# Attention scores from two fp32r parts of q and k in place of fp32 operands

## The chip, the cores and the metric

The kernel runs on one core of one Trainium2 chip. The metric is the device time of one execution in microseconds (us). The engines are TensorE (PE, with its weight loads listed apart as PEld), VectorE (DVE), ScalarE (ACT), GpSimd (POOL) and SyncE (SP), which here only issues DMAs. Each engine works through its own instructions in order.

## What is computed

Attention over 4 batches, 8 heads, 576 positions and a head size of 64, followed by a feed-forward layer over the 2304 tokens (512 to 2048 to 512).

```python
scores = q @ k.T / sqrt(64)
scores = scores + bias[head]          # a small network of log1p(|i-j|)/log1p(max(i,1)), one per head
attn = exp(scores - max) / (sum + 1e-9)
x = attn @ v                          # then laid out as 2304 x 512
h = x @ w_in
out = (s * relu(h)**2 + b) @ w_out    # w_in, w_out come as 64-bit floats
```

Everything is float32. The inputs q, k, v, w1, b1, w2 and w_in are drawn 8 times larger than the reference first draws them.

## The kernel before, in words

The order of all instructions is written out by hand (`tc.manual_schedule()`): what stands later in the program stands later in its engine's queue. There are three stages.

**Bias.** 36 steps compute the biases of 16 rows each, for all heads. The features of step st + 2 are issued ahead of step st (L118 is POOL's part of them), PE sums them (L135, L138), ACT evicts them (L142) and SP stores them to DRAM (L143). A table, `plan`, adds loads to single steps: among others q and k of pair 1 at step 6, q of pair 2 at step 20 and k of pair 2 at step 23. At steps 33 and 35 it starts the first two score units. Before those, the last biases are loaded back (L161, L162, L164), and SP waits there until their stores have landed.

**Attention.** The work is cut into 16 pairs: one head and two batches, whose 64-row q and k lie on partitions 0 to 63 and 64 to 127 of one tile (`qt`, `kt`, 128x640). A pair has five units. Units 0 to 3 are 128 query rows of both batches: `scores` (L196) makes four matmuls, two halves of 288 keys for each batch on its own 64 rows of the array. Unit 4 holds the last 64 rows of both batches and makes two matmuls on all 128 rows. The scores lie in a ring of two PSUM tiles (`sps`).

`step(n)` runs a pipeline of two units and one pair. In program order: scores and bias (DVE, L212) of unit n+2; the divisors of unit n+1 on DVE (L231, L232) and its scaling on POOL (`norm_scale`, L237); the transposes of unit n on PE (L259, L250, or L268, L263 in unit 4), which wait for that scaling, each evicted by ACT (L260, L255) or DVE (L257, L265); the exponentials of unit n+2 on ACT (L221); a fifth of attn @ v of the pair before (L283, L286); and, from pair 1 on, one `fill()`. Then come loads: q and k three pairs ahead at unit 3 (L171, L177), v at unit 4, and biases at unit 2 of every second pair.

`fill()` takes the next piece of decoding one weight block. A block has five pieces and a pair five steps, so the pieces keep their places. At unit 0: for the blocks that are split at once, a cast on DVE (L341) and a subtraction on POOL (L344), both of the block before, and then the absolute value on ACT (L322). At unit 1: a clip on POOL (L324). At units 2 to 4: DVE (L326, L329, L332). The blocks split at once are the first eight, so L344 runs in pairs 2 to 9.

**Feed-forward.** x and the weights are split into two fp32r parts, and expand (L379) and project (L408) sum three fp32r passes: high x high, high x low and low x high. During the first 512 tokens the rest of the weights is decoded.

The change touches `load_q`, `load_k`, `scores`, `step` and `plan`.

Of the kernel before, what the change touches and what calls it, by code (L numbers as in the profile page):

```python
# [9 lines left out]
F32 = mybir.dt.float32  # L10
F32R = mybir.dt.float32r
I32 = mybir.dt.int32
U32 = mybir.dt.uint32
AF = mybir.ActivationFunctionType
ALU = mybir.AluOpType
# [11 lines left out]
def attention_moe(ctx, tc, q, k, v, w_in, w_out, dist, par, out):  # L27
    nc = tc.nc
    NB, H, S, D = 2 * q.shape[0], q.shape[1], k.shape[3] - 64, q.shape[2] // 2
# [4 lines left out]
    HALF = S // 2  # L34
# [6 lines left out]
    NP = len(pairs)  # L41
    LAST = 5 * NP
# [7 lines left out]
    io = prep_ctx.enter_context(tc.tile_pool(name="io", bufs=2))  # L50
# [100 lines left out]
    qs, ks, vals, tts, bts, pts, units, accs = {}, {}, {}, {}, {}, {}, {}, {}  # L151
# [15 lines left out]
    def load_q(p):  # L167
        if p < NP:
            h, b0 = pairs[p]
            qs[p] = io.tile([128, 640], F32, tag="qt", name="qt", bufs=3)  # L170
            nc.sync.dma_start(out=qs[p], in_=q[b0 // 2, h])  # L171

    def load_k(p):
        if p < NP:
            h, b0 = pairs[p]
            ks[p] = io.tile([128, S + 64], F32, tag="kt", name="kt", bufs=3)
            nc.sync.dma_start(out=ks[p], in_=k[b0 // 2, h])  # L177

    def load_v(p):
        if p < NP:  # L180
            h, b0 = pairs[p]
            vt = tp.tile([128, 10 * D], F32, tag="vn", name="vt")
            nc.sync.dma_start(out=vt, in_=v[b0 // 2, h])
            vals[p] = vt.rearrange("p (i d) -> p i d", d=D)

    def scores(n):
        p, t = divmod(n, 5)
        qt, kt = qs[p], ks[p]
        c = slice(128 * t, 128 * t + 128)
        xs = range(width(n))  # L190
        ps = [ps_s.tile([128, 2, 512], F32, tag="s", name="sps") for _ in xs]
        for hf in range(2):
            for x in xs:
                d = slice(64 * x, 64 * x + 64) if t < 4 else slice(0, 128)
                o = hf * HALF + (64 if x == 0 else 0)
                nc.tensor.matmul(  # L196
                    ps[x][:, hf, 0:HALF], qt[d, c], kt[d, o:o + HALF], start=True, stop=True)
        units[n] = (
            tp.tile([128, 2, S], F32, tag="pr", name="pr"),
            sm.tile([128, 2], F32, tag="mn", name="mn"),  # L200
            sm.tile([128, 2], F32, tag="su", name="su"),
            sm.tile([128, 2], F32, tag="rs", name="rs"),
            ps,
        )

    def biased(n, x):
        p, t = divmod(n, 5)
        _, mn, _, _, ps = units[n]
        bt, be = bts[group[p]]
        bias = bt[:, t, 64 - 64 * x:64 - 64 * x + S] if t < 4 else be  # L210
        tt = tp.tile([128, S], F32, tag="tt", name="tt")
        nc.vector.tensor_tensor_reduce(  # L212
            tt.rearrange("p (a b) -> p a b", a=2), ps[x][:, :, 0:HALF],
            bias.rearrange("p (a b) -> p a b", a=2),
            -1.0 / ROOT, BIG, ALU.add, ALU.min, mn[:, x:x + 1],
        )
        tts[n, x] = tt

    def expo(n, x):
        pr, mn, su, _, _ = units[n]  # L220
        nc.scalar.activation(  # L221
            pr[:, x], tts.pop((n, x)), AF.Exp, bias=mn[:, x:x + 1], scale=-1.0,
            accum_out=su[:, x:x + 1])

    def width(n):
        return 2 if n % 5 < 4 else 1

    def norm(n):
        _, _, su, rs, _ = units[n]
        c = slice(0, width(n))  # L230
        nc.vector.tensor_scalar(su[:, c], su[:, c], 1e-9, None, op0=ALU.add)  # L231
        nc.vector.reciprocal(rs[:, c], su[:, c])  # L232

    def norm_scale(n, x):
        pr, _, _, rs, _ = units[n]
        r = rs[:, x:x + 1]
        nc.gpsimd.tensor_scalar(pr[:, x], pr[:, x], r, 1.0, op0=ALU.mult, op1=ALU.mult)  # L237

    def probs_t(n, part):
        p, t = divmod(n, 5)  # L240
        pr = units[n][0]
        if p not in pts:
            pts[p] = (ptp.tile([128, 4, 2, S], F32, tag="pt", name="pt"),
                      ptp.tile([128, S], F32, tag="ptr", name="ptr"))
        pt, ptr = pts[p]
        ps = ps_t.tile([128, 512], F32, tag="t", name="tps")
        c = slice(128 * t, 128 * t + 128)
        if t < 4 and part < 2:
            for kb in range(4):
                nc.tensor.transpose(  # L250
                    ps[:, 128 * kb:128 * kb + 128],
                    pr[:, part, 64 * part + 128 * kb:64 * part + 128 * kb + 128], ident)
            o, i = pt[:, :, part, c], ps.rearrange("p (a b) -> p a b", a=4)
            if part == 0:
                nc.scalar.activation(o, i, AF.Copy)  # L255
            else:
                nc.vector.tensor_copy(o, i)  # L257
        elif t < 4:
            nc.tensor.transpose(ps[:, 0:128], pr.rearrange("p x j -> p (x j)")[:, 512:640], ident)  # L259
            nc.scalar.activation(ptr[:, c], ps[:, 0:128], AF.Copy)  # L260
        elif part == 0:
            for kb in range(4):
                nc.tensor.transpose(  # L263
                    ps[:, 128 * kb:128 * kb + 128], pr[:, 0, 128 * kb:128 * kb + 128], ident)
            nc.vector.tensor_copy(  # L265
                pt[:, :, :, 512:S], ps.rearrange("p (a x b) -> p a x b", a=4, x=2))
        else:
            nc.tensor.transpose(ps[0:64, 0:128], pr[:, 0, 512:S], ident)  # L268
            for x in range(2):
                nc.scalar.activation(  # L270
                    ptr[64 * x:64 * x + 64, 512:S], ps[0:64, 64 * x:64 * x + 64], AF.Copy)

    def av(p, kb, hf):
        h, b0 = pairs[p]
        pt, ptr = pts[p]
        vt = vals[p]
        if kb == 0 and hf == 0:
            accs[p] = ps_x.tile([128, 2, 512], F32, tag="x", name="xps")
        ps = accs[p]
        c = slice(hf * HALF, (hf + 1) * HALF)  # L280
        if kb < 4:
            for x in range(2):
                nc.tensor.matmul(ps[64 * x:64 * x + 64, hf, 0:HALF], vt[:, 4 * x + kb, :], pt[:, kb, x, c],  # L283
                                 start=(kb == 0), stop=False)
        else:
            nc.tensor.matmul(ps[:, hf, 0:HALF], vt[:, 8:10].rearrange("p i d -> p (i d)"), ptr[:, c],  # L286
                             start=False, stop=True)
        if kb == 4 and hf == 1:
            xs = tp.tile([128, S], F32, tag="xs", name="xs", bufs=1)
            nc.scalar.activation(xs.rearrange("p (a b) -> p a b", a=2), ps[:, :, 0:HALF], AF.Copy)  # L290
            nc.sync.dma_start(out=xt_d[b0 // 2][:, h * D:(h + 1) * D, :], in_=xs)
# [130 lines left out]
    def ok(n, x):  # L422
        return 0 <= n < LAST and x < width(n)
# [7 lines left out]
    def step(n):  # L431
        p, u = divmod(n, 5)
        m = n + 2
        cur = 0 <= n < LAST
        if ok(m, 0):
            scores(m)
            biased(m, 0)
        if ok(n + 1, 0):
            norm(n + 1)
            norm_scale(n + 1, 0)  # L440
            if ok(n + 1, 1):
                norm_scale(n + 1, 1)
        if ok(m, 1):
            biased(m, 1)
        if cur:
            for part in (2, 0, 1) if u < 4 else (1, 0):
                probs_t(n, part)
        if ok(m, 0):
            expo(m, 0)
        if ok(m, 1):  # L450
            expo(m, 1)
        if p >= 1:
            av(p - 1, u, 0)
            av(p - 1, u, 1)
            fill()
        if n < LAST:
            if u == 3:
                load_q(p + 3)
                load_k(p + 3)
            if u == 4:  # L460
                load_v(p + 2)
            for e in loads_at.get((p, u), ()):
                load_bias(*e)
# [14 lines left out]
    def fill():  # L478
        next(filler, None)
# [10 lines left out]
        6: ((load_q, 1), (load_k, 1)),  # L490
        11: ((load_bias, 0, 0, 1),),
        17: ((load_bias, 0, 1, 2),),
        20: ((load_v, 0), (load_q, 2)),
        23: ((load_k, 2), (load_v, 1)),
        26: ((load_bias, 0, 2, 3),),
        29: ((load_w, *early[0]),),
        32: ((load_w, *early[1]),),
# [41 lines left out]
    for n in range(LAST - 2):  # L539
        step(n)  # L540
        if n >= LAST - 10:
            fill()
        if n == LAST - 4:
            for _ in filler:
                pass
            for a in range(KB):
                load_x(0, a)
    prep_ctx.close()
    xp = ctx.enter_context(tc.tile_pool(name="xp", bufs=1, reuse_waits="tile"))
    op = ctx.enter_context(tc.tile_pool(name="op", bufs=2, reuse_waits="tile"))  # L550
# [24 lines left out]
    for i in range(2, len(todo) + LAG):  # L575
        if i < len(todo):
            c, f = todo[i]
# [83 lines left out]
```

## Time and profile before

| | us |
|---|---|
| median of three runs (766.27 to 768.84) | 767.32 |
| the profiled execution | 769.54 |
| its span, first to last instruction | 767.8 |
| bias stage and its loads, until the scores go on | 0 to 73.2 |
| attention, pairs of 17.17 each | 73.2 to about 322 |
| end of attention and first tokens of the feed-forward | about 322 to 421 |
| the other tokens | 421 to 767.8 |

A row of the page of groups reads: line, engine, operation, output and inputs by the program's names, shapes, count, then busy time and mean nanoseconds of one, then the idle time of the engine right before them and what ended it. A row of a timeline reads: start and length in us, engine, line, operation, count, and in brackets the idle time before it with its releaser. In the chain of waits a row is start, length and what held the end back then. The chain goes by what came last, so an engine can be on it for long and still be closely followed by another.

### The profile page before, as it was taken

What the parts mean: (1) busy time and instruction counts of PE and PEld (TensorE: products, weight loads), DVE (VectorE), ACT (ScalarE), POOL (GpSimd) and SP (SyncE); (2) the same over time, 40 slices, a digit from 0 to 9 for tenths busy, and PEclk for the clock granted to TensorE, in tenths of its full rate; (3) what the DMA queues carried; (4) which work ended last, traced back from release to release, by engine and by line L of the source; (5) the groups of instructions that cost most, each with busy time, mean ns of one, the idle gap of its engine ahead of it and who ended that gap; (6) DMA issues with size and microseconds to landing.
All of it is one profiled execution on the core that took longest, in us unless ns stands there. A gap on an engine that the chain in (4) does not pass through costs nothing.

```text
span 767.8 us, 11563 instructions
## 1 busy us (share of the span) xinstructions
PE 735.5 (96%) x4226; PEld 528.1 (69%) x4226; DVE 433.3 (56%) x874; ACT 383.5 (50%) x788; POOL 242.8 (32%) x290
## 2 busy tenths in 40 slices
PE   8985999999999999999887999999999999999998
PEld 4443566666666666657655888888888888888896
DVE  7973678778777777866888432223322323223332
ACT  7983667777666677765454432223222323222332
POOL 7952345455554444438867310000000000000000
PEclk9997999999999999999989999999999999999999
DMA  5896243535444541252333003000300002000100
GB/s 173 285 335 195 81 161 112 175 126 195 156 155 141 182 143 61 76 172 79 110 123 89 10 15 95 1 0 1 107 4 1 1 0 83 1 0 1 56 1 27
DMA packets 36056, 71.56 MB, mean 93 GB/s; under 512 B 7712, under 2 KB 10912, under 8 KB 36000
## 3 DMA queue, kind: packets, MB, share of 16 engines
q1 hardware_dynamic: 35856, 70.51, 27.8%
q8 instruction: 33, 0.54, 0.3%
q10 hardware_dynamic: 144, 0.33, 0.1%
q14 instruction: 23, 0.19, 0.1%
HBM read 50.77 MB, written 20.05 MB: 92 GB/s over the span
## 4 chain that ended last, share of the span: by engine, by line
PE 80%; DMA 5%; POOL 4%; DVE 4%; issue 3%; ACT 3%; SPq 0%; ACTq 0%; POOLq 0%; DVEq 0%
PE o L408 23%; PE hps L379 22%; PE sps L196 12%; PE xps L283 8%; PE tps L250 8%; PE bps L135 2%; DMA bias<-stg 2%; PE xps L286 2%; PE tps L259 2%; POOL gt L391 2%; ACT stg L142 1%; DMA be<-bias 1%; DVE full L326 1%; DMA xt<-xs 1%; POOL full L324 1%
## 5 line engine op out<-in xcount | busy, mean ns | idle before, releaser
L408 PE MATMUL o<-who,gt 128*128 128x512 f32 x576 | 196.6, 401 | 12.6 <-ACT gt L390 8.9
L379 PE MATMUL hps<-x,whi 128*128 128x512 f32 (+1 forms) x640 | 184.4, 373 | 0.0
L384 DVE SCALAR_TENSOR_TENSOR r<-r,sb 128x512 f32<-128x512 f32 (+1 forms) x80 | 63.2, 790 | 182.9 <-ACT r L383 182.9
L237 POOL TENSOR_SCALAR pr<-pr,rs 128x576 f32<-128x576 f32 x144 | 108.8, 768 | 152.9 <-DVE rs L232 96.6
L383 ACT ACTIVATE r<-hps 128x512 f32<-128x512 f32 (+1 forms) x80 | 44.4, 554 | 191.3 <-PE hps L379 191.1
L408 PEld LDWEIGHTS o<-who,gt 128*128 128x128 f32 x576 | 109.5, 191 | 42.0 <-ACT gt L390 11.1
L379 PEld LDWEIGHTS hps<-x,whi 128*128 128x128 f32 x640 | 117.2, 188 | 24.4 <-issue 0.4
L212 DVE CUSTOM_DVE_ANT_0 tt<-sps,bt 128x576 f32<-128x576 f32 x128 | 95.8, 749 | 43.8 <-PE sps L196 42.2
L379 PE MATMUL hps<-x,wli 128*128 128x512 f32 (+1 forms) x320 | 118.8, 371 | 0.0
L221 ACT ACTIVATE pr<-tt,mn 128x576 f32<-128x576 f32 x144 | 110.2, 768 | 14.8 <-DVE su L231 12.2
L196 PE MATMUL sps<-kt,qt 64*128 64x288 f32 (+1 forms) x576 | 107.9, 437 | 9.8 <-DVE mn L212 9.4
L408 PE MATMUL o<-wlo,gt 128*128 128x512 f32 x288 | 114.5, 398 | 0.0
L196 PEld LDWEIGHTS sps<-kt,qt 64*128 64x128 f32 (+1 forms) x576 | 61.2, 189 | 52.0 <-DVE mn L212 21.0
L250 PE MATMUL tps<-ident,pr 128*128 128x128 f32 x512 | 76.7, 282 | 0.0
L283 PE MATMUL xps<-pt,vt 128*64 128x288 f32 x512 | 75.8, 418 | 0.0
L394 DVE SCALAR_TENSOR_TENSOR gt<-r,sb,gt 128x512 fp32r<-128x512 f32 (+1 forms) x64 | 43.8, 684 | 47.3 <-ACT gt L393 47.3
L379 PEld LDWEIGHTS hps<-x,wli 128*128 128x128 f32 x320 | 60.2, 188 | 11.1
L393 ACT ACTIVATE gt<-r,sb 128x512 fp32r<-128x512 f32 (+1 forms) x64 | 42.9, 670 | 48.2 <-DVE r L384 48.2
L250 PEld LDWEIGHTS tps<-ident,pr 128*128 128x128 f32 x512 | 57.7, 142 | 12.1 <-ACT ptr L260 10.5
L408 PEld LDWEIGHTS o<-wlo,gt 128*128 128x128 f32 x288 | 55.0, 191 | 11.5
L283 PEld LDWEIGHTS xps<-pt,vt 128*64 128x64 f32 x512 | 31.2, 136 | 23.9 <-issue 10.8
L257 DVE COPY pt<-tps 128x512 f32<-128x512 f32 x64 | 43.9, 687 | 3.5 <-PE tps L250 3.3
(66 smaller groups left out, 751.3 us busy)
## 6 DMA issues: line engine op xcount, KB each, us to landing
bias<-stg SPq DMA_DIRECT2D x36, 288.0 KB, 4.0
raw<-in_moe_w_in_dram SPq DMA_DIRECT2D x16, 512.0 KB, 3.5
raw<-in_moe_w_out_dram SPq DMA_DIRECT2D x16, 512.0 KB, 8.6
bt<-bias SPq DMA_DIRECT2D x7, 1152.0 KB, 12.7
qt<-in_q_dram SPq DMA_DIRECT2D x16, 320.0 KB, 10.2
kt<-in_k_dram SPq DMA_DIRECT2D x16, 320.0 KB, 10.5
vt<-in_v_dram SPq DMA_DIRECT2D x16, 320.0 KB, 9.3
xt<-xs SPq DMA_DIRECT2D x16, 288.0 KB
```

Of the source, the lines that this page charges most:

```text
L196: nc.tensor.matmul(ps[x][:, hf, 0:HALF], qt[d, c], kt[d, o:o + HALF], start=True, stop=True)
L212: nc.vector.tensor_tensor_reduce(tt.rearrange("p (a b) -> p a b", a=2), ps[x][:, :, 0:HALF], bias.rearrange("p (a b) -> p a b", a=2), -1.0 ...
L221: nc.scalar.activation(pr[:, x], tts.pop((n, x)), AF.Exp, bias=mn[:, x:x + 1], scale=-1.0, accum_out=su[:, x:x + 1])
L237: nc.gpsimd.tensor_scalar(pr[:, x], pr[:, x], r, 1.0, op0=ALU.mult, op1=ALU.mult)
L250: nc.tensor.transpose(ps[:, 128 * kb:128 * kb + 128], pr[:, part, 64 * part + 128 * kb:64 * part + 128 * kb + 128], ident)
L257: nc.vector.tensor_copy(o, i)
L283: nc.tensor.matmul(ps[64 * x:64 * x + 64, hf, 0:HALF], vt[:, 4 * x + kb, :], pt[:, kb, x, c], start=(kb == 0), stop=False)
L379: nc.tensor.matmul(ps[:, 0:n], w[0, g][:, a, fc], xs_t[c, a][:, j, 0:n], start=(i == 0), stop=(i == 3 * KB - 1))
L383: nc.scalar.activation(r, ps[:, 0:n], AF.Relu)
L384: nc.vector.scalar_tensor_tensor(r, r, sb[:, 0:1], r, op0=ALU.mult, op1=ALU.mult)
L394: nc.vector.scalar_tensor_tensor(lo, r, sb[:, 1:2], hi.bitcast(F32), op0=ALU.add, op1=ALU.subtract)
L408: nc.tensor.matmul(os_t[c][i], gt[:, a, tok], w[1, g][:, fo], start=(f == 0 and j == 0), stop=(f == NF - 1 and j == 2))
```

## The change

Each pair's q and k are split after their load. ScalarE copies the tile as fp32r (the high part), and GpSimd subtracts the copy from the tile (the low part). The two parts lie in one tile of twice the size. `scores` makes three fp32r matmuls (high x high, high x low, low x high) in place of each fp32 matmul, ordered by half, then by pass, then by batch, so that neighbouring matmuls are on different 64 rows. The splits of pair p+1 stand at the end of the steps of units 0 (q) and 1 (k) of pair p, and those of pair 0 behind bias steps 30 and 31. The loads of q and k come two pairs ahead with two buffers, not three with three, and so leave bias steps 20 and 23.

```diff
+    def split_qk(p, which):
+        if p < NP:
+            full = (qs, ks)[which][p]
+            t = io.tile([128, 2, 640], F32R, tag=f"r{which}", name="qr" if which == 0 else "kr")
+            nc.scalar.activation(t[:, 0], full, AF.Copy)
+            nc.gpsimd.tensor_tensor(t[:, 1], full, t[:, 0].bitcast(F32), op=ALU.subtract)
+            (qs, ks)[which][p] = t
...
+        mms = []
         for hf in range(2):
             for x in xs:
                 d = slice(64 * x, 64 * x + 64) if t < 4 else slice(0, 128)
                 o = hf * HALF + (64 if x == 0 else 0)
-                nc.tensor.matmul(
-                    ps[x][:, hf, 0:HALF], qt[d, c], kt[d, o:o + HALF], start=True, stop=True)
+                for i, (a, b) in enumerate(((0, 0), (0, 1), (1, 0))):
+                    mms.append((i, hf, x, ps[x][:, hf, 0:HALF], qt[d, a, c], kt[d, b, o:o + HALF]))
+        for i, _, _, o, a, b in sorted(mms, key=lambda e: e[1::-1]):
+            nc.tensor.matmul(o, a, b, start=(i == 0), stop=(i == 2))
...
-        if n < LAST:
+        if 0 <= n < LAST:
             if u == 3:
-                load_q(p + 3)
-                load_k(p + 3)
+                load_q(p + 2)
+                load_k(p + 2)
+            if u < 2:
+                split_qk(p + 1, u)
...
-        20: ((load_v, 0), (load_q, 2)),
-        23: ((load_k, 2), (load_v, 1)),
+        20: ((load_v, 0),),
+        23: ((load_v, 1),),
+        30: ((split_qk, 0, 0),),
+        31: ((split_qk, 0, 1),),
```

The tiles `qt` and `kt` also go from three buffers to two.

## Rows read from the trace of the kernel before

**Rows 1.** The page: busy tenths of PE and POOL and the granted clock of PE, each in 40 slices of the span.

```profile
PE   8985999999999999999887999999999999999998
...
POOL 7952345455554444438867310000000000000000
PEclk9997999999999999999989999999999999999999
```

**Rows 2.** Busy time of the engines in stretches: a pair with the POOL subtraction of the weights, a pair without it. Columns: stretch, its length, then each engine's busy time and instructions, granted clock, DMA share and GB/s.

```profile
218.84:236.01 17.17, 17.17 (x115) 10.63 (x114) 13.58 (x38) 12.08 (x32) 8.69 (x12) 1.00 0.35 122
...
270.34:287.51 17.17, 17.17 (x115) 10.63 (x114) 12.83 (x37) 12.05 (x32) 7.41 (x11) 1.00 0.37 129
```

**Rows 3.** The chain of waits in the first of these pairs: its first line (shares of the stretch), and score blocks of 64 rows (x8) and of 128 rows (x4).

```profile
by line: PE sps L196 37.9%; PE xps L283 26.1%; PE tps L250 23.8%; PE xps L286 7.1%; PE tps L259 5.2%; PE tps L263 2.5%; PE tps L268 1.3%
...
222.63 1.17 PE sps L196 x8
...
226.21 1.17 PE sps L196 x4
```

**Rows 4.** The timeline of PE in the same pair: the first transposes of units 0 to 3, and of unit 0 of the next pair.

```profile
220.16 0.33 PE L259 MATMUL tps<-ident,pr 128*128 128x128 f32 x1
...
223.73 0.33 PE L259 MATMUL tps<-ident,pr 128*128 128x128 f32 x1
...
227.21 0.27 PE L259 MATMUL tps<-ident,pr 128*128 128x128 f32 x1
...
230.73 0.33 PE L259 MATMUL tps<-ident,pr 128*128 128x128 f32 x1
...
237.33 0.33 PE L259 MATMUL tps<-ident,pr 128*128 128x128 f32 x1
```

**Rows 5.** Three-pass fp32r blocks of the feed-forward: the chain of waits with 512 columns a pass and with 256.

```profile
425.51 2.79 PE hps L379 x12
...
713.45 1.42 PE hps L379 x12
```

**Rows 6.** The groups by line: weight loads of the fp32r passes, and the transposes' own, with what they waited for.

```profile
L379 PEld LDWEIGHTS hps<-x,whi 128*128 128x128 f32 x640 | 117.2, 188 | 24.4 <-issue 0.4
...
L259 PEld LDWEIGHTS tps<-ident,pr 128*128 128x128 f32 x64 | 8.9, 139 | 22.2 <-POOL pr L237 16.4 <-issue 5.0
```

**Rows 7.** The timeline of POOL from unit 0 of that pair on: scaling of a unit (two instructions), the subtraction of a weight block, scaling of unit 2, the clip, scaling of unit 3, and the scaling ahead of the next pair.

```profile
221.62 1.47 POOL L237 TENSOR_SCALAR pr<-pr,rs 128x576 f32<-128x576 f32 x2 [1.69 <-ACT pt L255]
223.46 1.28 POOL L344 TENSOR_TENSOR wlo<-full,who 128x512 fp32r<-128x512 f32 x1 [0.36 <-DVE who L341]
225.22 1.47 POOL L237 TENSOR_SCALAR pr<-pr,rs 128x576 f32<-128x576 f32 x2 [0.49 <-ACT pt L255]
226.78 0.61 POOL L324 TENSOR_SCALAR full<-full 128x512 f32<-128x512 f32 x1
228.72 1.63 POOL L237 TENSOR_SCALAR pr<-pr,rs 128x576 f32<-128x576 f32 x2 [1.33 <-ACT pt L255]
...
235.64 1.47 POOL L237 TENSOR_SCALAR pr<-pr,rs 128x576 f32<-128x576 f32 x2 [2.84 <-DVE rs L232]
```

**Rows 8.** Two lines that split weights, all their instructions: duration in ns, shortest, median and longest, first and last start. The first is POOL's subtraction, the second ACT's fp32r copy.

```profile
L344 POOL TENSOR_TENSOR wlo<-full,who x16: 1275/1295/1749, 172.0 to 406.0; 128x512 fp32r<-128x512 f32 x16
...
L343 ACT ACTIVATE who<-full x12: 618/624/638, 354.0 to 404.0; 128x512 fp32r<-128x512 f32 x12
```

**Rows 9.** The timeline of ACT in that pair: the absolute value at unit 0, and the first eviction of unit 1.

```profile
222.97 0.67 ACT L322 ACTIVATE full<-raw 128x512 f32<-128x512 f32 x1
224.10 0.28 ACT L260 ACTIVATE ptr<-tps 128x128 f32<-128x128 f32 x1 [0.46 <-PE tps L259]
```

**Rows 10.** The timeline of SP at the end of the bias stage: loads of q and k of pair 2, the store of bias step 33, the stores of steps 34 and 35, the load that waits for them.

```profile
37.03 0.48 SPq L171 DMA_DIRECT2D qt<-in_q_dram  x1
...
40.12 1.13 SPq L177 DMA_DIRECT2D kt<-in_k_dram  x1
...
53.80 1.20 SPq L143 DMA_DIRECT2D bias<-stg  x1
...
57.98 1.17 SPq L143 DMA_DIRECT2D bias<-stg  x2
62.63 0.62 SPq L164 DMA_DIRECT2D be<-bias  x1
```

**Rows 11.** Other engines at that place: the last features on POOL, the evictions of bias steps 34 and 35 on ACT, and PE around its longest wait.

```profile
42.51 5.88 POOL L118 TENSOR_SCALAR f<-ls,thr 128x576 f32<-128x576 f32 x8
...
52.05 1.80 ACT L142 ACTIVATE stg<-bps,kc,pt__94 128x576 f32<-128x576 f32 x2 [0.45 <-ACT pr L221]
...
73.16 2.29 PE L196 MATMUL sps<-kt,qt 64*128 64x288 f32 x6 [7.61 <-DVE mn L212]
...
81.65 1.24 PE L196 MATMUL sps<-kt,qt 64*128 64x288 f32 x6 [0.27 <-DVE mn L212]
```

**Rows 12.** The load of q in a pair that also loads biases (timeline of SP), and the time from issue to landing of all loads of q.

```profile
207.40 2.90 SPq L164 DMA_DIRECT2D be<-bias  x1
210.39 3.81 SPq L171 DMA_DIRECT2D qt<-in_q_dram  x1
...
DMA to landing us min/median/max: 6.8/10.2/13.5
```

More of the change, by code (lines that the diff above doesn't have):

```diff
@@ L169, in load_q @@
             h, b0 = pairs[p]
-            qs[p] = io.tile([128, 640], F32, tag="qt", name="qt", bufs=3)
+            qs[p] = io.tile([128, 640], F32, tag="qt", name="qt")
             nc.sync.dma_start(out=qs[p], in_=q[b0 // 2, h])
@@ L175, in load_k @@
             h, b0 = pairs[p]
-            ks[p] = io.tile([128, S + 64], F32, tag="kt", name="kt", bufs=3)
+            ks[p] = io.tile([128, S + 64], F32, tag="kt", name="kt")
             nc.sync.dma_start(out=ks[p], in_=k[b0 // 2, h])
+    def split_qk(p, which):
[5 more added lines that the diff above has]
+            (qs, ks)[which][p] = t
     def load_v(p):
```

## The prediction, made before the change was run

> **What bounds the kernel now.** I read the page's slices first, then the busy times by stretch, then the chain of waits and the timelines of one pair. PE is busy at nine tenths from the third slice on [rows 1], and in a pair of the attention it is busy for all of its 17.17 us, while DVE, ACT and POOL are at 13.6, 12.1 and 8.7 [rows 2]. The chain in such a pair names PE alone; the scores hold 38% of it [rows 3]. So shorter scores should pay. The timelines correct this: PE waits at each unit's first transposes (L259) for POOL's scaling of that unit (L237), 16.4 us in all [rows 6], and at the pair's turn POOL ends at 235.64 + 1.47 = 237.11 while PE starts at 237.33 [rows 4, 7]. POOL is idle for half the time and yet follows PE closely: what counts is not its share but what stands ahead of a scaling in its queue.
>
> **Scores on PE.** A block of 64-row tiles has eight instructions (two for each fp32 matmul) and takes 1.17 us; a block on all rows has four and takes 1.17 too [rows 3]. So the two batches' tiles run side by side, and one instruction reads its 288 columns twice. After the change a tile has six passes of 288 columns read once. Blocks of twelve fp32r passes take 2.79 us with 512 columns and 1.42 with 256 [rows 5], 0.2325 and 0.118 each, so 0.1325 for 288. Six are 0.80 where four fp32 instructions take at least 4 x 0.24 (288 columns twice at 2.4 GHz, the granted 1.00 of rows 2), at most 4 x 0.265 (twice 0.1325). A block gets 0.17 to 0.27 shorter; I take 0.18, since 0.24 leaves 0.2 of the 1.17 for the first weights and the drain. Unhidden, that is 5 x 0.18 = 0.9 us a pair.
>
> **Splits on POOL.** The subtraction has the form of L344: 1.28 us for 512 elements, 1.76 at worst [rows 8]. For 640: at least 1.28 (nothing scales), at most 1.76 x 1.25 = 2.2; I take 1.55, just under 1.28 x 1.25, near the median. The Trainium skill ("GPSIMD Engine Reference", section Performance versus the Vector engine) gives 4497 ns for a two-input operation on 2048 elements, 2.2 ns each. By it 640 would take an estimated 1.41 us, and the two subtractions of 14 pairs would cost 4 us less in the sum below; the row has 1.28 for 512, or 2.5 ns each, and I keep to the row.
>
> The place matters more than the price. In program order the subtraction of q stands behind unit 0's fill and ahead of the scaling of unit 2, that of k ahead of the scaling of unit 3. In the pair of rows 4 and 7, with L344 in it:
> - L344 ends at 223.46 + 1.28 = 224.74. ACT's copy is there by then: its absolute value ends at 223.64 [rows 9], and a copy of 640 takes at most 0.62 x 1.25 = 0.78 [rows 8].
> - q's subtraction to 226.29, scaling of unit 2 (1.47) to 227.76. PE starts 0.22 behind the scaling, as at 237.33: at 227.98, not 227.21. It is 0.77 late.
> - Clip 0.61 to 228.37, k's subtraction to 229.92, scaling of unit 3 (1.63, as there) to 231.55, PE at 231.77, not 230.73: 1.04 late. Two scalings of 0.75 take 1.47, so neighbours overlap a little; I take 0.1 off. What PE saved in the scores of these steps is gone, for POOL sets both starts.
> - From unit 3 to unit 4 PE sets the pace again: 0.18 gained. At the pair's turn POOL has the last word already, so nothing is gained.
>
> That makes 0.94 - 0.18 = +0.76 us. Without L344 the subtraction starts at about 224.5, behind the copy: 0.24 earlier, +0.52. L344 runs in pairs 2 to 9: 8 x 0.76 = 6.1. Pairs 1 and 10 to 14: 6 x 0.52 = 3.1. Pair 15 splits nothing and gains 4 x 0.18 = 0.7. Pair 0 waits for biases anyhow. Each 0.1 us of the subtraction's length is worth 2 x 14 x 0.1 = 2.8 us.
>
> **Splits on ACT.** Some 0.75 us twice a pair, at units 0 and 1. ACT has 0.46 us free before unit 1's first eviction at 224.10 [rows 9], so this comes 0.3 to 0.5 late and holds PE's second group of transposes. That lies inside the 0.77 for which PE waits at unit 2, so I cost it at nothing; with POOL out of the way it would cost up to 0.5 a pair, 7 us.
>
> **Loads.** ACT's copy waits for the load of q. Where biases are loaded too, SP reaches q only at 210.39, behind the bias load that it issues from 207.40 on, and not because of the scores [rows 12]; at 10.2 to 13.5 us to landing that is 220.6 to 223.9, and the copy one pair on is due at 223.64 plus the pair's own lengthening. Just in time: nothing, at most 0.3 us in seven pairs.
>
> **Bias stage.** Two subtractions (3.1 us) join POOL's last features, which end at 48.4, and two copies join ACT [rows 11]. The stores of steps 34 and 35 are evicted by 53.85 but issued only at 57.98, since SP is behind; PE then waits 7.6 us for the load issued at 62.63 [rows 10, 11]. So up to 4 us of delay are covered. SP loses two loads, 0.58 (0.48 and a gap) + 1.13 = 1.7 us of its queue [rows 10]. Between +3.1 and -1.7 I take -1.0.
>
> **Sum.** 6.1 + 3.1 - 0.7 - 1.0 = +7.5. The profiled execution took 769.5 us, 2.2 above the median of the runs; the changed kernel's would take 777, and the median goes from 767.3 to 775.
>
> **Rivals.**
> *The splits hide (faster).* If POOL's subtractions stood behind the scalings of units 2 and 3, they would fill its idle time: 8.7 + 3.1 of 17.17 us [rows 2]. Then four steps of five gain 0.18 over 15 pairs, -10.8, and with the stage before 756. It decides at the arrival of PE: the scaling of unit 2 has to end 0.22 before 227.0. Against it: rows 7 have L344 between two scalings just where the program has it, and the order is written by hand.
> *The parts cancel.* Subtractions at 1.3 us give back 7 us: 768.
> *The tiles don't run side by side in fp32r, or their weights aren't hidden.* No row has fp32r on 64 rows. Twelve passes in a row are 1.59 where 0.80 was; the block grows by 0.6, 3 us a pair, +46 over 15 pairs: 813. With each pass's weights exposed (0.11, the difference of 1.17 and four times 0.265) a block is 6 x 0.24 + 0.1 and grows by 0.4: +28, 795. Against the second: the 256-column passes come every 0.118 us though each has a weight load of 0.188 on the same rows [rows 5, 6].
> The Trainium skill ("TensorE: Matmul & The Clock Gate", Part 3: Packing small matmuls) says that weight loads overlap running matmuls only on other row groups. By that rule it would be the 795; these rows speak against it.
> *The clock.* After PE's 7.6 us wait six score instructions took 2.29 us, not 1.24, and were back at 1.24 by 81.65 [rows 11]: half clock for some 8 us, 4 lost. Waits of 0.8 us are far shorter; but if each pair paid this, it would be +56: 831.
>
> **Chances.** The forecast 0.70; its own range, by the bounds of the subtraction (1.28 to 2.2: -7.6 to +18) and of the bias stage, is 766 to 795, and a tenth of the chance in it lies within 0.3% of before. Hidden splits 0.16, cancelling 0.05, tiles or weights 0.06, clock 0.03. A run can tell 0.3%, some 2.3 us, from no change. Faster: 0.16. Same: 0.05 + 0.08 = 0.13. Slower: 0.71. Of the range 765 to 795 the 756 is left out, and most of the two last.
>
> **What would show it.** In the trace of after: POOL's subtractions of 128x640 ahead of the scalings of units 2 and 3; transposes of these two units released by POOL, later by 0.8 and 0.9 us; score blocks of about 1.0 us; pairs of 17.9 us up to pair 9, 17.7 then, and about 16.5 for the last. I am wrong if PE is still busy for the whole pair (then the scores set the time, and their block tells by how much), or if the scalings run ahead of the subtractions.

## The result and the profile after

The changed kernel takes 777.82 us (median of four runs, 777.33 to 778.85) where the kernel before, on the same chip, takes 767.33: a ratio of 1.0141 [1.0125, 1.0158]. The profiled execution took 778.85 us with a span of 776.9, against 769.54 and 767.8 before.

The page of the changed kernel: busy tenths of PE and POOL and the granted clock in 40 slices, and the shares of the chain of waits.

```profile
PE   9986999999999989899888899999999999999998
...
POOL 7974566666666555636877410000000000000000
PEclk9996999999999999999989999999999999999999
...
PE 55%; POOL 14%; DVE 11%; DMA 10%; issue 7%; ACT 3%; POOLq 0%; ACTq 0%; DVEq 0%; SPq 0%
```

Beside [rows 1], POOL has gone from four or five tenths to five or six in the attention, far from full, while PE now has eights in it, and the chain has POOL in it for a seventh. One pair, the same as in [rows 2], shows it closer (stretch, length, busy time and instructions of each engine, granted clock, DMA share, GB/s):

```profile
223.78:241.62 17.84, 16.67 (x133) 11.19 (x132) 14.15 (x38) 13.25 (x33) 11.56 (x13) 1.00 0.33 113
```

A pair takes 17.84 us, not 17.17. PE has less to do in it (16.67) and stands still for 1.17. The timeline of PE in this pair has score blocks, the first transposes of units 1 to 4 and of the next pair (unit 0 starts at 223.78), and one later group of transposes (L261):

```profile
226.18 1.07 PE L208 MATMUL sps<-kr,qr 64*128 64x288 f32 x12
227.17 0.33 PE L270 MATMUL tps<-ident,pr 128*128 128x128 f32 x1
...
228.18 0.66 PE L261 MATMUL tps<-ident,pr 128*128 128x128 f32 x4 [0.24 <-ACT ptr L271]
...
229.89 1.07 PE L208 MATMUL sps<-kr,qr 128*128 128x288 f32 x6
231.52 0.33 PE L270 MATMUL tps<-ident,pr 128*128 128x128 f32 x1 [0.56 <-POOL pr L248]
...
235.35 0.33 PE L270 MATMUL tps<-ident,pr 128*128 128x128 f32 x1 [0.36 <-POOL pr L248]
...
238.75 0.30 PE L279 MATMUL tps<-ident,pr 128*64 128x128 f32 x1
...
240.39 1.28 PE L208 MATMUL sps<-kr,qr 64*128 64x288 f32 x12
241.62 0.33 PE L270 MATMUL tps<-ident,pr 128*128 128x128 f32 x1
```

PE has three waits. Two are for POOL's scaling, ahead of units 2 and 3. The third, 0.24 us for ACT's eviction in unit 1, lies inside the time for which unit 2 has to wait for POOL anyway. Here is the timeline of POOL from unit 1's step on: weight subtraction, q's subtraction, scaling of unit 2, clip, k's subtraction, scaling of unit 3.

```profile
227.23 1.28 POOL L355 TENSOR_TENSOR wlo<-full,who 128x512 fp32r<-128x512 f32 x1 [0.36 <-DVE who L352]
228.47 1.54 POOL L184 TENSOR_TENSOR qr<-qt,qr 128x640 fp32r<-128x640 f32 x1
230.01 1.46 POOL L248 TENSOR_SCALAR pr<-pr,rs 128x576 f32<-128x576 f32 x2
231.55 0.61 POOL L335 TENSOR_SCALAR full<-full 128x512 f32<-128x512 f32 x1
232.13 1.56 POOL L184 TENSOR_TENSOR kr<-kt,kr 128x640 fp32r<-128x640 f32 x1
233.78 1.52 POOL L248 TENSOR_SCALAR pr<-pr,rs 128x576 f32<-128x576 f32 x2
```

The scalings end at 231.47 and 235.30, and PE starts 0.05 behind each. The groups by line, over the whole span, have the scores' matmuls (107.9 us of busy time before, in 576 instructions), the transposes with their wait, and three of the four new lines:

```profile
L208 PE MATMUL sps<-kr,qr 64*128 64x288 f32 (+1 forms) x864 | 92.3, 317 | 7.3 <-DVE mn L223 6.6 <-ACT stg L142 0.7
L184 POOL TENSOR_TENSOR qr<-qt,qr 128x640 fp32r<-128x640 f32 x16 | 24.8, 1552 | 12.3 <-ACT qr L183 10.7 <-DVE f L116 1.5
L184 POOL TENSOR_TENSOR kr<-kt,kr 128x640 fp32r<-128x640 f32 x16 | 24.8, 1552 | 0.0
...
L270 PE MATMUL tps<-ident,pr 128*128 128x128 f32 x64 | 21.2, 332 | 15.3 <-POOL pr L248 14.5
L183 ACT ACTIVATE qr<-qt 128x640 fp32r<-128x640 f32 x16 | 11.6, 726 | 1.9 <-DMA qt<-in_q_dram 1.9
```

The last row is a second wait: in three pairs ACT's copy waits for the load of q. ACT and PE in the worst of them, pair 12 (18.72 us long):

```profile
281.77 0.74 ACT L183 ACTIVATE qr<-qt 128x640 fp32r<-128x640 f32 x1 [1.20 <-DMA qt<-in_q_dram]
```

```profile
282.72 0.66 PE L261 MATMUL tps<-ident,pr 128*128 128x128 f32 x4 [1.54 <-ACT ptr L271]
```

The eviction of PE's transposes stands behind the copy in ACT's queue, so PE waits for the load too. At the end, pair 15 splits nothing and yet takes 14.55 us, not 13.51. PE in that pair, and then its busy time and clock in the stretch that follows the wait:

```profile
343.30 0.33 PE L270 MATMUL tps<-ident,pr 128*128 128x128 f32 x1 [1.67 <-POOL pr L248]
```

```profile
344.80:348.20 3.40, 3.40 (x15) 1.98 (x12) 3.30 (x6) 2.40 (x6) 0.00 (x0) 0.50 0.78 300
```

The granted clock is 0.50 (1.2 GHz) in this stretch, and unit 4 starts 3.26 us after unit 3. The wait alone does not bring this. In the traces of seven of the nine experiments below pair 15 has the same wait (1.67 to 1.69 us), PE goes on at the full clock, and unit 4 follows after 2.40 us, as in the kernel before. PE in the eighth, at units 3 and 4:

```profile
326.00 0.33 PE L279 MATMUL tps<-ident,pr 128*128 128x128 f32 x1 [1.67 <-POOL pr L257]
...
328.40 0.30 PE L288 MATMUL tps<-ident,pr 128*64 128x128 f32 x1
```

The account over the span of the profiled execution: pair 1 starts at 81.06 instead of 82.82, -1.8; pairs 1 to 9 are +6.0 (17.84 each but for the first, 17.82, against 17.17), pairs 10 to 14 +4.6 (two of them only +0.25, pair 11 +0.8, pair 12 +1.55, pair 14 +1.7), pair 15 +1.0, what follows -0.8. The sum, +9.0, is the 9.1 between the spans but for rounding. Of pair 15's +1.0, 0.86 is the half clock of this one execution.

### The profile page after: what moved, and what is told of

Its sections match the earlier page's. It is cut to its first block, busy times and chain, and to the rows that moved or that the text cites. A ratio compares the mean times of both kernels' runs of the same rounds, so it can differ in the third digit from the quotient of the medians.

```text
span 776.9 us, 12225 instructions
## 1 busy us (share of the span) xinstructions
PE 729.5 (94%) x4514; PEld 541.0 (70%) x4514; DVE 441.2 (57%) x874; ACT 401.1 (52%) x820; POOL 290.0 (37%) x322
## 4 chain that ended last, share of the span: by engine, by line
PE 55%; POOL 14%; DVE 11%; DMA 10%; issue 7%; ACT 3%; POOLq 0%; ACTq 0%; DVEq 0%; SPq 0%
PE o L419 22%; PE hps L390 21%; DMA qt<-in_q_dram 7%; POOL pr L248 5%; DVE tt L223 3%; PE bps L135 3%; PE sps L208 3%; PE tps L261 2%; PE xps L294 2%; POOL full L335 2%; POOL kr L184 2%; POOL gt L402 2%; DVE full L343 2%; POOL wli L355 1%; DMA be<-bias 1%
## 5 line engine op out<-in xcount | busy, mean ns | idle before, releaser
L232 ACT ACTIVATE pr<-tt,mn 128x576 f32<-128x576 f32 x144 | 110.7, 770 | 13.6 <-DVE su L242 9.2
L208 PEld LDWEIGHTS sps<-kr,qr 64*128 64x128 f32 (+1 forms) x864 | 71.4, 190 | 41.3 <-DVE mn L223 17.2
L208 PE MATMUL sps<-kr,qr 64*128 64x288 f32 (+1 forms) x864 | 92.3, 317 | 7.3 <-DVE mn L223 6.6
L261 PE MATMUL tps<-ident,pr 128*128 128x128 f32 x512 | 78.5, 284 | 5.9 <-ACT ptr L271 5.8
L261 PEld LDWEIGHTS tps<-ident,pr 128*128 128x128 f32 x512 | 58.5, 144 | 17.4 <-ACT ptr L271 17.4
```

The costliest lines, as they stand in the source:

```text
L208: nc.tensor.matmul(o, a, b, start=(i == 0), stop=(i == 2))
L232: nc.scalar.activation(pr[:, x], tts.pop((n, x)), AF.Exp, bias=mn[:, x:x + 1], scale=-1.0, accum_out=su[:, x:x + 1])
L261: nc.tensor.transpose(ps[:, 128 * kb:128 * kb + 128], pr[:, part, 64 * part + 128 * kb:64 * part + 128 * kb + 128], ident)
```

## Experiments

Two theories were put against each other: that POOL's two subtractions, because of where they stand in its queue, hold units 2 and 3; and that PE, ACT's copies or the loads cost the time. Diffs are against the changed kernel where nothing else is said. The expectations call the experiments e1 to e9, in the order in which they stand here. The kernel before took 766.55 to 766.83 us (medians of 11 to 14 runs) in their three series, 0.5 to 0.8 less than beside the changed kernel, and differences against the changed kernel's 777.82 can be off by that much.

**The subtractions away.** POOL's subtractions go; PE keeps its number of passes.

```diff
             nc.scalar.activation(t[:, 0], full, AF.Copy)
-            nc.gpsimd.tensor_tensor(t[:, 1], full, t[:, 0].bitcast(F32), op=ALU.subtract)
...
-                    mms.append((i, hf, x, ps[x][:, hf, 0:HALF], qt[d, a, c], kt[d, b, o:o + HALF]))
+                    mms.append((i, hf, x, ps[x][:, hf, 0:HALF], qt[d, 0, c], kt[d, 0, o:o + HALF]))
```

> The changed kernel without POOL's subtractions of q and k; all three passes of the scores read the high parts, so the low parts are left out of the computation. Loads, ScalarE's copies and the passes stay. Theory (the subtractions' place in POOL's queue sets the starts of units 2 and 3): pairs fall from 17.84 and 17.42 to about 16.5, unit 1 to unit 2 from 4.35 to 3.1 to 3.3, total 760 to 762. Rival (ScalarE's copies delay the transposes): pairs stay above 17.2, total within 5 us of 777.8. Rival (late loads of q): only pairs 11 and 12 matter, total unchanged here, as the loads stay.

Measured 769.17 us (766.54 to 771.43), ratio to before 1.0033 [1.0011, 1.0055]: 8.65 below the changed kernel, but not as far as expected. Half of the pairs take 16.62 us, as the first theory has it; six take 17.8 to 20.2. One of these, in the timelines of ACT and of PE, and PE's stretch behind the wait:

```profile
221.05 0.74 ACT L183 ACTIVATE qr<-qt 128x640 fp32r<-128x640 f32 x1 [1.24 <-DMA qt<-in_q_dram]
```

```profile
222.01 0.66 PE L260 MATMUL tps<-ident,pr 128*128 128x128 f32 x4 [1.60 <-ACT ptr L270]
222.59 2.12 PE L293 MATMUL xps<-pt,vt 128*64 128x288 f32 x8
```

```profile
222.70:226.10 3.40, 3.40 (x14) 2.06 (x15) 0.69 (x1) 1.88 (x5) 0.85 (x2) 0.50 0.47 180
```

With POOL out of the way the loads come to the front: pairs get shorter, and the copy of q waits for its load, 8.1 us in six pairs; in two of them the granted clock is 0.50 behind the wait. So POOL is the first cause and there is a second beneath it.

**The passes back to fp32.** The splits stay, and the scores are fp32 matmuls again.

```diff
-                for i, (a, b) in enumerate(((0, 0), (0, 1), (1, 0))):
-                    mms.append((i, hf, x, ps[x][:, hf, 0:HALF], qt[d, a, c], kt[d, b, o:o + HALF]))
+                mms.append((0, hf, x, ps[x][:, hf, 0:HALF], qt[d, 0, c].bitcast(F32), kt[d, 0, o:o + HALF].bitcast(F32)))
...
-            nc.tensor.matmul(o, a, b, start=(i == 0), stop=(i == 2))
+            nc.tensor.matmul(o, a, b, start=True, stop=True)
```

> The changed kernel with its splits, copies and loads, but with the scores in fp32 as before, on the high parts alone (the low parts are computed and left out of the scores). Theory: from unit 0 to unit 3 POOL sets the pace and nothing changes; unit 3 to 4 goes back to 3.57 and the pair's turn to 3.03, so pairs are 18.2 and the total is 782 to 784. Rival (PE sets the pace in all units): 5 x 0.18 us more in 15 pairs, pairs of 18.7, total 791.

Measured 782.36 us (781.54 to 784.99), ratio 1.0208 [1.0189, 1.0227]. PE in a pair that begins at 210.03:

```profile
217.62 0.33 PE L269 MATMUL tps<-ident,pr 128*128 128x128 f32 x1 [0.33 <-POOL pr L247]
...
221.47 0.33 PE L269 MATMUL tps<-ident,pr 128*128 128x128 f32 x1 [0.20 <-POOL pr L247]
...
228.07 0.33 PE L269 MATMUL tps<-ident,pr 128*128 128x128 f32 x1
```

PE does the same passes as before the change and waits for POOL at the same two units. The pair is 18.04 us, near the theory's 18.2, and the rival's 791 us is out: the splits alone cost 0.87, and the faster passes give back only 0.2 of that.

**The loads two units earlier.**

```diff
         if 0 <= n < LAST:
-            if u == 3:
+            if u == 1:
                 load_q(p + 2)
```

> The changed kernel with the loads of q and k issued at unit 1, ahead of the bias loads, and not at unit 3. Theory (late loads are a second, small cause): the ScalarE copy no longer waits for q in pairs 11 and 12, these fall to 17.4, total 775.5 to 776.5. Rival (the loads are hidden, the long pairs come from something else): no change, 777.8. Rival (q and k now delay the bias loads): slower than 777.8.

Measured 775.62 us (774.65 to 779.41), ratio 1.0126 [1.0104, 1.0148]. The group of ACT's copies of q no longer waits:

```profile
L183 ACT ACTIVATE qr<-qt 128x640 fp32r<-128x640 f32 x16 | 11.6, 724 | 0.0
```

Pairs 11 and 12 are back at 17.42, like 10 and 13, 0.56 and 1.30 less than in the changed kernel. Pair 14 is 20.0 here (18.89 there), since PE's granted clock is 0.50 behind its wait of 1.63 us, so in this execution not much of the gain is left. The medians differ by 2.2, but the two intervals overlap (the changed kernel's is 1.0125 to 1.0158): it is the two pairs, 1.86 us, that show the gain.

**The splits elsewhere.** Copy and subtraction of q at the end of unit 2's step, those of k at the end of unit 3's, two pairs ahead, with loads at unit 4 three pairs ahead.

```diff
-            if u == 3:
-                load_q(p + 2)
-                load_k(p + 2)
...
-            if u < 2:
+            if p < 2 and u < 2:
                 split_qk(p + 1, u)
+            if p > 0 and u in (2, 3):
+                split_qk(p + 2, u - 2)
+            if u == 4:
+                load_q(p + 3)
+                load_k(p + 3)
```

The loads of pair 2 stay at unit 3 of pair 0, and the split tiles get three buffers.

> The changed kernel with the splits at the ends of units 2 and 3, two pairs ahead, where POOL has least to do, with loads at unit 4, three pairs ahead, and three buffers for the split tiles; the splits of pairs 1 and 2 stay where they were. Nothing is left out. Theory: the subtractions fill POOL's idle time and the shorter scores count: pairs of 16.4, total 752 to 757. Rival (what a split costs is its work on POOL and ScalarE, wherever it stands): pairs of 17.4 to 17.8, total 772 to 778. Rival (the place moves the stall): units 3 or 4 grow by over 0.5 us, total 760 to 770.

Measured 782.75 us (780.89 to 784.66), ratio 1.0207 [1.0186, 1.0228]: almost 26 us above the range of the theory. The first three periods of a pair are as expected (in one, unit starts at 119.89, 123.27 and 126.67, 3.4 apart), but then, in the timelines of SP and of ACT:

```profile
116.91 0.52 SPq L302 DMA_DIRECT2D xt<-xs  x1
117.52 0.91 SPq L171 DMA_DIRECT2D qt<-in_q_dram  x1
```

```profile
128.57 0.74 ACT L183 ACTIVATE qr<-qt 128x640 fp32r<-128x640 f32 x1 [3.15 <-DMA qt<-in_q_dram]
```

At unit 4 the load stands behind the store of x in SP's queue, ahead of which SP issues nothing from 108.27 to 116.91. It starts at 117.52 and lands 11.05 us later, and unit 2 is there by then: unit 4 starts at 132.23, 5.56 behind unit 3. The group of copies waits for q for 24.2 us in twelve pairs. PE's waits at units 2 and 3 are gone, but the total says nothing on the place of the subtractions, since I had moved the loads as well.

**The first experiment with the early loads.** The edit of the first, and loads at unit 1.

> As e1 (no subtractions on POOL, all three passes on the high parts, the low parts left out), with the loads of q and k at unit 1, ahead of the bias loads, as in e3. Theory (behind POOL's subtractions stands a second wait of the same place, ScalarE's copy waiting for q, which showed in six pairs of e1): all pairs 16.6, total 769.2 - 12 = 757, within 2. Rival (the long pairs of e1 have another cause, the half clock seen in two of them): these pairs stay long, total 765 to 769.

Measured 759.27 us (757.41 to 760.34), ratio 0.9900 [0.9879, 0.9921]. A pair by its stretch, and PE in it:

```profile
213.65:230.27 16.62, 16.36 (x132) 11.20 (x132) 13.94 (x38) 13.29 (x33) 8.69 (x11) 1.00 0.37 124
```

```profile
218.06 0.66 PE L260 MATMUL tps<-ident,pr 128*128 128x128 f32 x4 [0.26 <-ACT ptr L270]
```

Pairs 1 to 14 all take 16.5 to 16.7 us. Here the passes bring 0.55 us a pair against [rows 2], and it would be more if ACT's copy did not hold PE's second group of transposes for 0.26 us a pair. Subtractions and late loads together are thus worth 18.55 us of the changed kernel's time, late loads alone about 2 (the third experiment).

**The splits elsewhere, with early loads.** Both copies and q's subtraction at the end of unit 2's step, k's subtraction behind POOL's scaling in unit 3's step; loads three pairs ahead at unit 1.

```diff
+            if p > 0 and u == 3:
+                split_lo(p + 2, 1)
...
-            if u == 3:
-                load_q(p + 2)
-                load_k(p + 2)
...
-            if u < 2:
+            if p < 2 and u < 2:
                 split_qk(p + 1, u)
+            if p > 0 and u == 1:
+                load_q(p + 3)
+                load_k(p + 3)
+            if p > 0 and u == 2:
+                split_qk(p + 2, 0)
+                split_hi(p + 2, 1)
```

`split_hi` is the copy of `split_qk`, `split_lo` its subtraction; the first two lines stand right behind `norm_scale`, and pair 0 loads and splits as in the fourth.

> As e4, splits two pairs ahead where POOL is idle, nothing left out, but with both ScalarE copies and q's subtraction at the end of unit 2, k's subtraction right behind the scaling in the step of unit 3, and the loads of q and k three pairs ahead at unit 1, ahead of the bias loads and of the store of the pair's result. Theory (e4 lost its gain to loads stuck behind that store, and to k's subtraction ahead of the scaling of the next pair's unit 0): pairs of 16.2 to 16.6 throughout, total 752 to 757. Rival (in POOL's and ScalarE's queues there is no room for the splits at any place): pairs of 17.2 and more, total 765 or more.

Measured 762.83 us (762.06 to 765.56), ratio 0.9952 [0.9936, 0.9969]: faster than before, yet not the 752 to 757. In pairs 2 to 13 units follow at 3.4 us, and PE does not wait for POOL, but the turn to the next pair takes 3.43 instead of 2.87. DVE, POOL and PE at that place:

```profile
211.27 1.83 DVE L349 SCALAR_TENSOR_TENSOR full<-raw,full 128x512 uint32<-128x512 uint32 x1
```

```profile
211.00 1.56 POOL L189 TENSOR_TENSOR kr<-kt,kr 128x640 fp32r<-128x640 f32 x1
```

```profile
214.78 1.06 PE L217 MATMUL sps<-kr,qr 64*128 64x288 f32 x11 [0.39 <-DVE mn L232]
```

The decoding piece takes 0.68 us in the kernel before. Here it takes 1.83 and ends 0.5 us behind POOL's subtraction; DVE's bias of the next scores (L232) stands behind it, and PE waits for that.

**The same places with fp32 passes.** The sixth kernel with the edit of the second.

> As e6, but with the scores in fp32 on the high parts (the low parts are computed and left out of the scores). Theory (in e6 the splits are hidden, and its gain is that of the passes on PE alone): pairs of 17.2 as before the change, total 765 to 768. Rival (e6 gains from the loads or the order, not from the passes): well below 765, near e6.

Measured 771.78 us (770.35 to 773.01), ratio 1.0063 [1.0044, 1.0082]: far above the sixth kernel, as the theory has it, but over its 768. A pair, and DVE in it:

```profile
217.19:234.73 17.54, 17.54 (x115) 10.66 (x114) 14.58 (x38) 13.33 (x32) 11.70 (x14) 1.00 0.36 124
```

```profile
233.53 1.76 DVE L348 SCALAR_TENSOR_TENSOR full<-raw,full 128x512 uint32<-128x512 uint32 x1
```

A pair has 0.37 us more than before, all at the turn (3.40 where the kernel before has 3.03). So the hold of DVE is there with either kind of passes (with fp32r passes the turn has 0.56 more than 2.87), and the passes alone, with POOL not in their way, bring 771.78 - 762.83 = 8.95 us. At the change's own places they brought 782.36 - 777.82 = 4.5.

**Both subtractions at unit 2.** Against the sixth kernel, k's subtraction goes to the end of unit 2's step, behind q's.

```diff
-            if p > 0 and u == 3:
-                split_lo(p + 2, 1)
...
                 split_qk(p + 2, 0)
-                split_hi(p + 2, 1)
+                split_qk(p + 2, 1)
```

> As e6, nothing left out, but with k's subtraction right behind q's at the end of unit 2, ahead of the scaling of unit 4. Theory (in e6 VectorE's piece of decoding at unit 3 is held until POOL's subtraction of k ends, 1.8 us for 0.69, and this makes the pair's turn 3.45 for 2.87): the hold shrinks to some 0.4 us, the turn goes to 2.9 to 3.0, unit 3 to unit 4 grows by some 0.2, pairs of 16.5 to 16.7, total 757 to 760. Rival (the turn is long for POOL's own queue, not for VectorE): with the scaling of unit 4 behind two subtractions pairs stay at 17.0 or more, total 763 or more.

Measured 761.25 us (759.76 to 762.10), ratio 0.9935 [0.9922, 0.9948]: the lowest median of a kernel that has the whole split, 16.6 us below the changed one, and just above the range of the theory. Its interval overlaps with the sixth's, but its pairs are 16.72 us and not 17.00. A pair, then POOL in it:

```profile
214.51:231.23 16.72, 16.13 (x134) 11.04 (x132) 14.04 (x38) 13.22 (x33) 12.12 (x13) 1.00 0.37 124
```

```profile
222.72 1.63 POOL L257 TENSOR_SCALAR pr<-pr,rs 128x576 f32<-128x576 f32 x2 [1.10 <-ACT pt L275]
224.31 1.55 POOL L189 TENSOR_TENSOR qr<-qt,qr 128x640 fp32r<-128x640 f32 x1
225.83 1.55 POOL L189 TENSOR_TENSOR kr<-kt,kr 128x640 fp32r<-128x640 f32 x1
227.36 1.18 POOL L257 TENSOR_SCALAR pr<-pr,rs 128x576 f32<-128x576 f32 x1
```

POOL is busy for 12.12 us of the pair, more than in the changed kernel (11.56), and the pair is only 0.1 us longer than without subtractions (16.62). Unit 4, whose scaling is one instruction and not two, starts late behind the two subtractions (4.05 us after unit 3), and the turn takes 2.63 instead of 2.87.

**k's subtraction at unit 4.** Against the sixth kernel, it goes one step later.

```diff
-            if p > 0 and u == 3:
+            if p > 0 and u == 4:
                 split_lo(p + 2, 1)
```

> As e6, nothing left out, but with k's subtraction one unit later, right behind the scaling in the step of unit 4. Theory (it is the hold of VectorE that costs in e6): the decoding at unit 3 is back at 0.69 us, the pair's turn at 2.87; the subtraction now meets the decoding and the divisors at the turn, which costs up to 0.2, pairs of 16.4 to 16.6, total 755 to 759. Rival (POOL's queue): the scaling of unit 1 starts behind the subtraction and pairs stay at 16.9 or more, total 762 or more.

Measured 764.55 us (763.38 to 765.45), ratio 0.9971 [0.9958, 0.9984]. The turn is 2.86, and the decoding piece 0.68 us again; that much was right. But POOL, and then DVE, at the next unit:

```profile
217.34 1.98 POOL L189 TENSOR_TENSOR kr<-kt,kr 128x640 fp32r<-128x640 f32 x1
219.74 1.46 POOL L257 TENSOR_SCALAR pr<-pr,rs 128x576 f32<-128x576 f32 x2 [0.43 <-ACT pr L241]
```

```profile
218.50 0.84 DVE L251 TENSOR_SCALAR su<-su 128x2 f32<-128x2 f32 x1
```

The subtraction now runs beside DVE's divisors of unit 1, which take 0.84 us where 0.16 would do, and unit 1's scaling starts late: the first two periods are 3.84 and 3.59, and the pair 17.09. The total is the one that the rival named, but not by its cause, since POOL is idle for 0.43 us ahead of that scaling. The hold was not avoided, only moved.

## Why the prediction was right, and where it was not

The forecast of 775.0 us is 2.8 below the measured 777.82, in range and sign, and by the cause it gave. Two rows of the kernel before are needed for this: the score block at the turn, and the transposes in the groups by line (matmuls, where [rows 6] has their weight loads).

```profile
235.94 1.46 PE L196 MATMUL sps<-kt,qt 64*128 64x288 f32 x8
...
L259 PE MATMUL tps<-ident,pr 128*128 128x128 f32 x64 | 20.3, 317 | 2.0 <-POOL pr L237 2.0
```

The steps of the forecast:

- *Score blocks shorter by 0.18.* Right: 1.07 us, for both kinds of block, by the same view as the 1.24 before. The passes on 64 rows run side by side: twelve take as long as six on all rows.
- *POOL's subtraction 1.55 us.* Right: 1.552, both lines. The Trainium skill ("GPSIMD Engine Reference", section Performance versus the Vector engine) led to an estimate of 1.41; the scaling of the row by its elements was nearer.
- *Units 2 and 3 late by 0.77 and 0.94.* The place was right, and the removal of the subtractions showed it. From the start of the pair, unit 2 comes after 7.74 us (7.05 in [rows 4]) and unit 3 after 11.57 (10.57): 0.69 and 1.00 late. The pair comes to +0.67, not 0.76, for the reason in the next point. Pairs 1 to 9 were forecast at 6.6 in all and have 6.0.
- *The turn: "nothing is gained".* This step failed. I read POOL's end at 237.11 and PE's start at 237.33 [rows 4, 7] as a hand-over of 0.22 us; the row of PE has no bracket, that is, no wait, and hand-overs that are waited for took 0.05. POOL was early there, and PE was set by its own score block (1.46 us in that place before, 1.28 after). The turn gained 0.16: 2.87 where 3.03 was. In the same way the 16.4 us of [rows 6] were the idle time of the weight load; the matmuls of that line waited for POOL for 2.0 us in the kernel before and for 14.5 in the changed one. The forecast lost only the 0.16 us a pair, as it went by the times at which POOL ends. In pairs 10 and 13, which have no subtraction of weights, unit 3 is 0.58 late, not 0.70, and with the turn's 0.16 they have +0.25 and +0.23 where 0.52 was forecast.
- *Loads: "nothing, at most 0.3 in seven pairs".* Mis-sized. The copy waited in three pairs, 1.9 us in all, and pairs 11 and 12 are 0.56 and 1.3 longer than their neighbours; the early loads removed just these. I bounded the landing by a pair with POOL's weight subtraction, where POOL holds everything long enough. Where pairs are shorter the load comes late; without the subtractions (first experiment) it was the next bound, for half of the gain.
- *ACT's copies hidden under POOL's wait, up to 0.5 a pair without it.* Right in both halves: the 0.24 us of the changed kernel lie inside POOL's wait, and 0.26 a pair counted once POOL was out of the way.
- *Pair 15: "gains 4 x 0.18".* Failed: +1.04. Its scores are shorter, but the step that waits for POOL (1.33 us before, 1.67 after) takes the time back: in the seven traces with the full clock there, pair 15 has 13.67 to 13.71 us where 13.51 was. The other 0.86 (3.26 us to unit 4, where 2.40 was) is the half clock behind the wait, which came in this execution and not in those seven, so nothing ties it to the change. The 16.5 us that the prediction names for the last pair start from a full pair of 17.17, which this one never was (it has no turn). Pair 14, where two decoding pieces a step begin, has +1.7 where 0.52 was forecast. In it POOL's clip, the second piece, stands between q's subtraction and the scaling of unit 2, and this scaling takes 2.13 us, not 1.46, so unit 2 starts 1.74 late; without the subtractions (fifth experiment) the pair has 16.67 us. Why the scaling takes longer was not tried.
- *Bias stage -1.0.* It was -1.8: the load that waits for the stores was issued at 61.67, not 62.63, which is 1.0 of it; the rest I did not trace.

So +7.5 was forecast and +9.1 measured between the spans: 0.6 too much for pairs 1 to 9, 0.8 too much for the bias stage, 2.0 too little for pairs 10 to 14, 1.7 too little for pair 15, and that what follows got 0.8 shorter was not forecast. The errors are 3.7 one way and 2.2 the other, so that the sum came so close is in part luck. The rest of the 2.8 is the step from the profiled execution to the median, taken as 2.2 and measured as 1.0.

Of the rivals, hidden splits was wrong for this order of the program and nearly right for another: it gave 756 us, and the kernel with both subtractions behind the scaling of unit 3 takes 761.25. That fp32r tiles do not run side by side, or that their weights are exposed, is refuted by the 1.07 us block. The Trainium skill ("TensorE: Matmul & The Clock Gate", Part 3: Packing small matmuls) has weight loads overlap running matmuls only on other row groups. The 795 that the prediction took from this does not follow for units 0 to 3, whose neighbouring passes are on different 64 rows; what does not agree with the rule is the block of unit 4, six passes on the same 128 rows in 1.07 us, where exposed weights would have made it about 1.5 by the prediction's sum. The clock rival did not happen in an ordinary pair, whose waits are 0.66 us at most; at the end it happened in this execution, but not in seven others with the same wait.

## What to carry to other kernels

An engine that is idle for half of the time can set the pace: ask what stands ahead of the one instruction that another engine waits for, and put new work behind it, in the gap that its timeline shows. A timeline's gap between two engines is a wait only where the waiting row says so. When one wait is removed, look at once for the next: here it was the load of q, and beneath that DVE beside POOL.

## What the runs showed of the hardware

- **Some DVE operations stand still beside a two-input operation of POOL.** The decoding piece (two inputs in SBUF) took 0.68 us alone and 1.83 beside k's subtraction. The first operation of the divisors (L231 before, L242 after), 0.16 us for two elements a partition, took up to 1.56; its mean over the span went from 174 to 275 ns with the change. The Trainium skill ("GPSIMD Engine Reference", section Specifications) says that POOL shares its interfaces to SBUF with VectorE and contends with instructions of two SBUF inputs or in a two-port mode; the decoding piece agrees with it. Which of the two the divisors meet, no run here shows. Not every operation was held: the reciprocal behind the divisors kept its 0.17 us, and DVE's operations that read PSUM their 0.7. And a one-input operation of POOL does it too, but less: beside a scaling, the last decoding piece (L332) took 1.01 us in the kernel before, where 0.69 would do.
- **A wait of 1.6 us can be followed by the half clock, and need not be.** PE's clock was 0.50 behind waits of 1.60 us (first experiment) and 1.67 (pair 15). It was 1.00 behind waits of 1.62 us (pair 14 of the same execution), 1.67 to 1.69 (pair 15 in seven experiments), 1.90 (first experiment) and 2.10 (fourth). So the length of the wait does not settle it, and what does, no run here shows. A wait that brings the half clock costs more than itself: eight matmuls behind it took 2.12 us in the first experiment, and 1.19 behind a wait of 1.54 us in pair 12 of the changed kernel, at the full clock.
